# Three engines held to the order of the program in the main part of the second feed-forward layer

## The chip, the cores and the metric

One core of one Trainium2 chip runs the kernel. The metric is the device time of one execution in microseconds (us); several executions are timed, and one more is profiled. TensorE multiplies matrices, VectorE and ScalarE work on rows of 128 partitions, GpSimd helps a little at the start, and SyncE issues the DMA transfers. In the profile these are PE (with PEld, the load of weights), DVE, ACT, POOL and SP.

## What is computed

The input is a causal attention with exponential decay (2 batches, 8 heads, 768 positions, head dimension 64). Its output, as 1536 tokens of 512 features, goes through two feed-forward layers with 2048 hidden features each:

```
h = x @ w_in                       # layer 1
g = h * tanh(softplus(h))          # Mish
x = g @ w_out
h = x @ w2_in                      # layer 2
g = h * clip(h + 3, 0, 6) / 6      # hard swish
out = g @ w2_out
```

All is float32; the kernel splits each operand into a high and a low part and multiplies three times.

## The kernel before

**Layer 2** is what the change touches. It has three blocks of 512 tokens (in the order 2, 0, 1) and eight feature pieces `p` of 256 for each, so 24 steps `j` = 0 to 23. Both matrix products use a 2 x 2 block scheme with seven products in place of eight, which adds sums on VectorE. One step is the loop body over `j`, and it has four parts `f` = 0 to 3:

- `fill` (L687): the products of the first matrix for part `f`, into a PSUM bank: 6 matmuls of 256 columns for part 0 and 12 for each other part. I call them fill a, b, c and d. In steps 0 and 1 two banks take turns; from step 2 on all four fills use **one bank**, number 0.
- the copy out of that bank on ScalarE (L802), called copy a, b, c and d. The next fill can start only when the copy has read the bank.
- adds on VectorE with that copy (L805 in part 1, L809 and L812 in part 2, L814 in part 3).
- `second(j - 2)` (L701): products of the second matrix for the step two earlier, into other banks: 6 matmuls in part 0, 12 in each other part. In steps 0 and 1 the last matmuls of layer 1 (L327) stand here, and VectorE adds their results to `part` (L365).

Between these stand, for the features of step `j - 1`:

- `gate` (L711 on ScalarE, a relu into a buffer `x`; L712 on VectorE). It comes twice a step: for two of the four features at the end of a step (part 3), for the other two in part 0 of the next step.
- `feature_sums` (L721): four sums on VectorE, in part 0.
- `feature_parts`: two splits, each a high part on ScalarE (L88) and a low part on VectorE (L91), of 768 and of 1024 columns, in part 1. `second` reads them one step later.

**Tokens.** The sums over the tokens of the next block are a generator `token_sums` with seven splits (`put`: L88 on ScalarE, L91 on VectorE, 512 columns) and four differences (L383 on VectorE). The program takes one item of it in part 1 and one in part 3 of each step, from step 0 on for block 0 and from step 9 on for block 1.

**Closing.** With the last piece of a block, `close` (L737 on ScalarE, L740 and L745 on VectorE) scales and adds the seven accumulators and stores the result. That is in steps 9 and 17, and after step 23.

**What sets the order.** The tile framework orders each engine's instructions itself, by what it takes to be ready first, and an instruction can so be put ahead of one that the program has before it. An instruction that goes through `tc.keep_in_program_order` keeps its place in the program on its engine. Before the change only some instructions of the start do so. Each engine runs its queue in the order in which it was built.

Of the kernel before, what the change touches and what calls it, by code (L numbers as in the profile page):

```python
# [20 lines left out]
def decay_attention__mish_ffn__hswish_ffn_kernel(  # L21
# [14 lines left out]
    NPAIR = NF // 2  # L36

# [49 lines left out]
    def split_hi(hi, src):  # L87
        nc.scalar.activation(out=hi, in_=src, func=ACTF.Copy)  # L88

    def split_lo(lo, hi, src):  # L90
        nc.vector.tensor_tensor(out=lo, in0=src, in1=f32(hi), op=ALU.subtract)  # L91
# [43 lines left out]
    def decay_tables():  # L135
        small = tm1_p.tile([128, 344], F32, tag="th", name="small")
        tc.keep_in_program_order(nc.sync.dma_start(out=small[:, 0:140], in_=lam))
        load_raw(0, 0)
        load_raw(0, 1)
        load_raw(1, 0)  # L140
        load_w(*plan[0])
        load_raw(1, 1)
        unit, zero = small[:, 12:140], small[:, 144:272]
        nc.vector.memset(zero, 0.0)
# [12 lines left out]

    def scores(c, kind):
        qT, kT = qk(c)
        sc = [bank(kind, [128, 4, 128]) for h2 in range(2)]  # L160
        for p in range(4):
            for h2 in range(2):
                r = slice(h2 * 64, h2 * 64 + 64)
                nc.tensor.matmul(sc[h2][:, p, :], lhsT=kT[r, p, :], rhs=qT[r, p, :], start=True, stop=True)  # L164
        sc_t[c] = sc
# [7 lines left out]
    def weigh(c):  # L173
        qT, kT = qk(c)
        kn, vn = kv(c)
        sc = sc_t.pop(c)
        if c < 4:
            if carries(c):
                kk = kn.rearrange("j (p h d) -> j p h d", p=4, h=2)
                nc.gpsimd.tensor_tensor(out=kk, in0=kk, in1=reverse(), op=ALU.mult)  # L180
            if follows(c):
                nc.gpsimd.tensor_tensor(out=qT, in0=qT, in1=lampow, op=ALU.mult)
        else:
            lo = 0 if follows(c) else 1
            hi = 2 if carries(c) else 1
            qkn = raw_t[c][:, 512 + 512 * lo:512 + 512 * hi].rearrange("p (n i) -> p n i", i=512)
            nc.vector.tensor_tensor(out=qkn, in0=qkn, in1=table[:, lo:hi], op=ALU.mult)
        for h2 in range(2):
            nc.vector.tensor_tensor(out=amat[h2], in0=sc[h2], in1=mask[:, h2], op=ALU.mult)  # L189

    def attend(c, kind):
        qT, kT = qk(c)
        kn, vn = kv(c)
        uo = [bank(kind, [128, 2, 256]) for i in range(2)]
        u = uo[0][:, 1].rearrange("p (a d) -> p a d", a=4)
        o = [b[:, 0].rearrange("p (a i) -> p a i", a=2) for b in uo]
        half = [slice(0, 64), slice(64, 128)]
        if carries(c):
            for p in range(4):
                for h2 in range(2):  # L200
                    s = slice(p * 128 + h2 * 64, p * 128 + h2 * 64 + 64)
                    nc.tensor.matmul(u[half[h2], p], lhsT=kn[:, s], rhs=vn[:, s], start=True, stop=True)
        last = not follows(c)
        for h2 in range(2):
            for a in range(2):
                for e in range(2):
                    p = 2 * a + e
                    s = slice(p * 128 + h2 * 64, p * 128 + h2 * 64 + 64)
                    nc.tensor.matmul(  # L209
                        o[h2][half[e], a], lhsT=vn[:, s], rhs=amat[h2][:, p, :],  # L210
                        start=(a == 0), stop=(last and a == 1), skip_group_check=True,
                    )
        if follows(c):
            for a in range(2):
                for e in range(2):
                    for h2 in range(2):
                        p = 2 * a + e
                        nc.tensor.matmul(  # L218
                            o[h2][half[e], a], lhsT=state[c % 2][half[h2], p, :], rhs=qT[half[h2], p, :],
                            start=False, stop=(a == 1), skip_group_check=True,  # L220
                        )
        uo_t[c] = u, o
        del raw_t[c]

    def settle(c):
        u, o = uo_t.pop(c)
        off = (c % 4) * 128

        def tokens():
            for h2 in range(2):  # L230
                kt = slice(2 * h2, 2 * h2 + 2)
                hi = X[c // 4][:, 0, kt, off:off + 128]
                split_hi(hi, o[h2])
                split_lo(X[c // 4][:, 1, kt, off:off + 128], hi, o[h2])

        if c == 3:
            tokens()
        if carries(c):
            new = state[(c + 1) % 2]
            if follows(c):  # L240
                nc.vector.tensor_tensor(out=new, in0=faded, in1=u, op=ALU.add)
            else:
                nc.vector.tensor_copy(new, u)
            if carries(c + 1):
                nc.gpsimd.tensor_tensor(
                    out=faded, in0=new, in1=lampow[:, :, 127:128].to_broadcast([128, 4, 64]), op=ALU.mult
                )
        if c != 3:
            tokens()
# [31 lines left out]
    def to_single(st, dest=None):  # L281
# [7 lines left out]
        nc.vector.scalar_tensor_tensor(  # L289
            out=lo, in0=hi, scalar=-2 ** 31, in1=lo, op0=ALU.bitwise_and, op1=ALU.bitwise_or  # L290
        )
        nc.vector.scalar_tensor_tensor(  # L292
            out=hi if dest is None else dest.bitcast(I32), in0=hi, scalar=3, in1=lo,
            op0=ALU.logical_shift_left, op1=ALU.bitwise_or
        )
# [19 lines left out]
    def gemm1(k, t, h):  # L315
        order = [(kt, a, 0) for kt in range(4) for a in range(2)] + [(kt, 0, 1) for kt in range(4)]
        for kt, a, b in order:
            nc.tensor.matmul(  # L318
                h, lhsT=W[t][:, a, kt * 128:kt * 128 + 128], rhs=X[k][:, b, kt, :],
                start=(kt, a, b) == order[0], stop=(kt, a, b) == order[-1],  # L320
            )

    def gemm2(layer, t, g, y, first, last, es):
        for e in es:
            for i, (a, b) in enumerate(PASS):
                l, r = W[t][:, a, 512 + e * 128:640 + e * 128], g[:, b, :]
                nc.tensor.matmul(  # L327
                    y[e], lhsT=l, rhs=r, start=(first and i == 0), stop=(last and i == 2),
                )
# [13 lines left out]
    def act_first(n):  # L343
# [3 lines left out]
        nc.scalar.activation(out=x, in_=h, func=ACTF.Mish)  # L347
        nc.scalar.activation(out=g[:, 0], in_=h, func=ACTF.Mish)  # L348
# [9 lines left out]
    def evacuate(n, es):  # L358
        layer, k, t, first, last, end = seq[n]
        for e in es:  # L360
            y = y_t[e]
            if end == "keep":
                nc.scalar.activation(out=part[k][:, e, :], in_=y, func=ACTF.Copy)
            elif end == "add":
                nc.vector.tensor_tensor(out=part[k][:, e, :], in0=part[k][:, e, :], in1=y, op=ALU.add)  # L365
        if end == "split":
# [3 lines left out]
            nc.scalar.activation(out=tmp[:, 0], in_=y[:, 0:2, 256:512], func=ACTF.Copy)  # L370
# [3 lines left out]
    def token_sums(k, y, tmp=None):  # L374
# [7 lines left out]
        def sub(o, a, b):  # L382
            nc.vector.tensor_tensor(out=o, in0=a, in1=b, op=ALU.subtract)  # L383
# [121 lines left out]
    def assemble(u):  # L505
# [4 lines left out]
        for o, x, y, op in WSUMS[half]:  # L510
            nc.vector.tensor_tensor(out=B[:, o], in0=B[:, x], in1=B[:, y], op=op)
# [29 lines left out]
    for c in range(4):  # L541
# [12 lines left out]
        else:  # L554
            nc.gpsimd.tensor_copy(table[:, 1].rearrange("j (p h d) -> j p h d", p=4, h=2), reverse())
# [123 lines left out]
    def fill(j, ms, bank_):  # L679
        k, p = runs[j]  # L680
        slot = slot_at[j][p, 0]
        for i, m in enumerate(ms):
            wi, xi = FIRST[m]
            w, x = operand(slot, wi), XC[k][xi]
            for kt in range(2):
                for q, (a, b) in enumerate(PASS):
                    nc.tensor.matmul(  # L687
                        bank_[:, 256 * i:256 * i + 256], lhsT=w[:, a, kt * 128:kt * 128 + 128], rhs=x[:, b, kt],
                        start=(i == 0 and kt == 0 and q == 0), stop=(kt == 1 and q == 2), skip_group_check=True,
                    )  # L690

    def second(j, ms):
# [3 lines left out]
        for m in ms:  # L696
            gi, wi = SECOND[m]
            w, acc = operand(slot, wi), BANK[:, ACC[m]].rearrange("p (s n) -> p s n", s=2)
            for i in range(2):
                for q, (a, b) in enumerate(PASS):  # L700
                    nc.tensor.matmul(  # L701
                        acc[:, i], lhsT=GB[j % 2][:, gi, a, i * 128:i * 128 + 128], rhs=w[:, b],
                        start=(first and i == 0 and q == 0), stop=(last and q == 2), skip_group_check=True,
                    )
# [3 lines left out]
    def gate(j, lo, step):  # L708
        F = FH[j % 2][:, lo:lo + step + 1:step]
        x = tm2_p.tile([128, 2, 256], F32, tag="x", name="x")  # L710
        nc.scalar.activation(out=x, in_=F, func=ACTF.Relu, bias=3.0)  # L711
        nc.vector.scalar_tensor_tensor(out=F, in0=x, scalar=6.0, in1=F, op0=ALU.min, op1=ALU.mult)  # L712

    def feature_sums(j):
        F, S = FH[j % 2], FS[j % 2]
        A21, A11, A22, A12 = (F[:, i] for i in range(4))
        for o, a, b, op in (
# [3 lines left out]
            nc.vector.tensor_tensor(out=S[:, o], in0=a, in1=b, op=op)  # L721
# [14 lines left out]
    def scaled(o, m):  # L736
        nc.scalar.activation(out=o, in_=BANK[:, ACC[m]], func=ACTF.Copy, scale=SIXTH)  # L737

    def added(o, m, b):
        nc.vector.scalar_tensor_tensor(  # L740
            out=o, in0=BANK[:, ACC[m]], scalar=SIXTH, in1=b, op0=ALU.mult, op1=ALU.add
        )

    def plus(o, a, b):
        nc.vector.tensor_tensor(out=o, in0=a, in1=b, op=ALU.add)  # L745
# [40 lines left out]

    GAPS = ((1,), (4, 2), (6, 7), (5, 3))
    prepare = []
    for j in range(R):
# [7 lines left out]
        for f, (name, ms) in enumerate(FILLS):  # L797
# [4 lines left out]
            nc.scalar.activation(out=c, in_=bank_[:, 0:n], func=ACTF.Copy)  # L802
            c = c.rearrange("p (i n) -> p i n", n=256)
            if f == 1:
                nc.vector.tensor_tensor(  # L805
                    out=F[:, 2:4], in0=COPY["a"].unsqueeze(1).to_broadcast([128, 2, 256]), in1=c, op=ALU.add
                )
            elif f == 2:
                nc.vector.tensor_tensor(  # L809
                    out=F[:, 0:4:3], in0=F[:, 3:4].to_broadcast([128, 2, 256]), in1=c, op=ALU.add  # L810
                )
                nc.vector.tensor_tensor(out=F[:, 1], in0=F[:, 0], in1=c[:, 1], op=ALU.add)  # L812
            elif f == 3:
                nc.vector.tensor_tensor(out=F[:, 0:4:3], in0=F[:, 0:4:3], in1=c, op=ALU.add)  # L814
# [78 lines left out]
```

## Time and profile before

| | |
|---|---|
| three timed runs | 573.69, 572.15 and 571.12 us, median 572.15 us |
| the profiled execution | 571.27 us, of which the span of the trace is 569.5 us |
| mean granted TensorE clock | 0.999 |
| layer 2, step 0 starts | 311.72 us |
| PE busy, all instructions | 554.4 us, 97% of the span |
| DVE, ACT busy | 433.9 us (76%), 320.1 us (56%) |

The span runs from the first to the last instruction of the trace; the rest of the 571.27 us lies around it.

### The profile page before, as it was taken

Reading aid. Unit: us, or ns where it says so; the run is one execution under the profiler, and the core shown is the slowest. Engines: PE = TensorE matmul, PEld = TensorE weight load, DVE = VectorE, ACT = ScalarE, POOL = GpSimd, SP = SyncE. Lnnn points to the kernel's source line nnn. Section 1 sums busy time; section 2 is a strip of 40 time slices with the busy share of each in tenths; the row PEclk is TensorE's granted clock in tenths of the full one; section 3 lists DMA queues with packets and bytes.
Section 4 is the critical chain, followed back from the end, with each engine's and each line's share of the span. In section 5 each row is a group of like instructions: output and inputs, shape, how many; then the busy total and the mean of one; then the engine's idle time right before and its main releaser. Section 6 shows DMA issues by size and latency. Waiting matters only on the chain.

```text
span 569.5 us, 9630 instructions
## 1 busy us (share of the span) xinstructions
PE 554.4 (97%) x3886; PEld 492.0 (86%) x3886; DVE 433.9 (76%) x667; ACT 320.1 (56%) x476; POOL 16.7 (3%) x20
## 2 busy tenths in 40 slices
PE   7799999999999999999999999999999999999996
PEld 4677787778888888888888999999999999999995
DVE  6899953475637888798997696689887776987765
ACT  1578733346754676676765464465555555555451
POOL 3500100000000000000000000000000000000000
PEclk9999999999999999999999999999999999999999
DMA  8966612522355797869969999894498885699902
GB/s 307 401 220 246 245 66 75 185 75 94 134 181 210 291 386 263 346 234 399 389 277 393 402 360 378 325 351 168 164 364 322 314 330 174 219 346 347 381 34 74
DMA packets 25260, 149.06 MB, mean 262 GB/s; under 512 B 2304, under 2 KB 5504, under 8 KB 18304
## 3 DMA queue, kind: packets, MB, share of 16 engines
q1 hardware_dynamic: 25216, 148.45, 68.7%
q8 instruction: 30, 0.49, 0.3%
q14 instruction: 14, 0.11, 0.1%
HBM read 115.94 MB, written 32.51 MB: 261 GB/s over the span
## 4 chain that ended last, share of the span: by engine, by line
PE 85%; DVE 7%; ACT 3%; DMA 3%; issue 1%; SPq 0%; DVEq 0%; ACTq 0%
PE bank L318 22%; PE bank L327 21%; PE bank L687 20%; PE bank L701 18%; DMA st<-w 1%; DMA ring<-w 1%; PE bank L164 1%; PE bank L209 1%; PE bank L218 1%; DVE st L289 1%; DVE ring L292 1%; DVE amat L189 1%; ACT st L286 1%; DVE rest L740 1%; DVE X L91 1%
## 5 line engine op out<-in xcount | busy, mean ns | idle before, releaser
L327 PE MATMUL bank<-g,up 128*128 128x512 f32 x288 | 70.3, 389 | 0.0
L318 PE MATMUL bank<-X,up 128*128 128x512 f32 x288 | 69.2, 389 | 0.0
L347 ACT ACTIVATE x<-bank 128x512 f32<-128x512 f32 x48 | 28.6, 595 | 63.6 <-PE bank L318 63.5
L318 PEld LDWEIGHTS bank<-X,up 128*128 128x128 f32 x288 | 54.1, 188 | 11.2
L327 PEld LDWEIGHTS bank<-g,up 128*128 128x128 f32 x288 | 53.5, 188 | 10.6
L687 PE MATMUL bank<-X,up 128*128 128x256 f32 x384 | 55.5, 286 | 0.6 <-ACT work L802 0.5
L91 DVE TENSOR_TENSOR g<-x,g 128x512 fp32r<-128x512 f32 x48 | 32.9, 686 | 28.9 <-ACT g L348 28.7
L712 DVE SCALAR_TENSOR_TENSOR work<-x,work 128x512 f32<-128x512 f32 x48 | 33.1, 690 | 26.4 <-ACT x L711 26.3
L711 ACT ACTIVATE x<-work 128x512 f32<-128x512 f32 x48 | 30.3, 632 | 40.6 <-DVE work L812 24.6
L687 PEld LDWEIGHTS bank<-X,up 128*128 128x128 f32 x384 | 49.6, 191 | 1.5 <-ACT work L802 1.0
L802 ACT ACTIVATE two<-bank 128x512 f32<-128x512 f32 x48 | 28.6, 597 | 34.0 <-PE bank L687 34.0
L286 ACT ACTIVATE ring<-ring 128x512 f32<-128x512 f32 (+3 forms) x52 | 39.9, 818 | 13.5 <-DMA ring<-w 12.9
L318 PE MATMUL bank<-X,lowA 128*128 128x512 f32 x180 | 45.2, 397 | 0.0
L327 PE MATMUL bank<-g,lowA 128*128 128x512 f32 x180 | 43.2, 389 | 0.0
L701 PE MATMUL bank<-up,lowB 128*128 128x256 f32 x318 | 42.9, 283 | 0.0
L701 PEld LDWEIGHTS bank<-up,lowB 128*128 128x128 f32 x318 | 40.2, 192 | 0.0
L318 PEld LDWEIGHTS bank<-X,lowA 128*128 128x128 f32 x180 | 33.0, 188 | 8.2 <-issue 1.2
L687 PE MATMUL bank<-X,lowA 128*128 128x256 f32 x270 | 38.9, 285 | 1.2 <-ACT work L802 1.1
L327 PEld LDWEIGHTS bank<-g,lowA 128*128 128x128 f32 x180 | 33.8, 188 | 7.1
L802 ACT ACTIVATE work<-bank 128x256 f32<-128x256 f32 (+1 forms) x48 | 23.5, 490 | 27.7 <-PE bank L687 27.4
L701 PE MATMUL bank<-up,up 128*128 128x256 f32 x276 | 37.7, 283 | 0.0
L687 PEld LDWEIGHTS bank<-X,lowA 128*128 128x128 f32 x270 | 35.1, 191 | 2.1 <-ACT work L802 1.8
(103 smaller groups left out, 1018.7 us busy)
## 6 DMA issues: line engine op xcount, KB each, us to landing
up<-wc SPq DMA_DIRECT2D x19, 1792.0 KB, 10.1
wc<-lowA SPq DMA_DIRECT2D x16, 1792.0 KB, 8.9
lowA<-wc SPq DMA_DIRECT2D x13, 1792.0 KB, 8.4
raw<-att SPq DMA_DIRECT2D x24, 512.0 KB, 6.4
ring<-w SPq DMA_DIRECT2D x18, 512.0 KB, 5.1
ring<-w SPq DMA_DIRECT2D x8, 1024.0 KB, 5.7
spare<-w SPq DMA_DIRECT2D x8, 1024.0 KB, 6.3
lowB<-wc SPq DMA_DIRECT2D x6, 1280.0 KB, 5.8
```

The costliest lines, as they stand in the source:

```text
L91: nc.vector.tensor_tensor(out=lo, in0=src, in1=f32(hi), op=ALU.subtract)
L164: nc.tensor.matmul(sc[h2][:, p, :], lhsT=kT[r, p, :], rhs=qT[r, p, :], start=True, stop=True)
L189: nc.vector.tensor_tensor(out=amat[h2], in0=sc[h2], in1=mask[:, h2], op=ALU.mult)
L286: ins = nc.scalar.activation(out=o, in_=i, func=ACTF.Copy, scale=scale, bias=bias)
L318: nc.tensor.matmul(h, lhsT=W[t][:, a, kt * 128:kt * 128 + 128], rhs=X[k][:, b, kt, :], start=(kt, a, b) == order[0], stop=(kt, a, b) == or ...
L327: nc.tensor.matmul(y[e], lhsT=l, rhs=r, start=(first and i == 0), stop=(last and i == 2),)
L347: nc.scalar.activation(out=x, in_=h, func=ACTF.Mish)
L687: nc.tensor.matmul(bank_[:, 256 * i:256 * i + 256], lhsT=w[:, a, kt * 128:kt * 128 + 128], rhs=x[:, b, kt], start=(i == 0 and kt == 0 and ...
L701: nc.tensor.matmul(acc[:, i], lhsT=GB[j % 2][:, gi, a, i * 128:i * 128 + 128], rhs=w[:, b], start=(first and i == 0 and q == 0), stop=(las ...
L711: nc.scalar.activation(out=x, in_=F, func=ACTF.Relu, bias=3.0)
L712: nc.vector.scalar_tensor_tensor(out=F, in0=x, scalar=6.0, in1=F, op0=ALU.min, op1=ALU.mult)
L802: nc.scalar.activation(out=c, in_=bank_[:, 0:n], func=ACTF.Copy)
```

## The change

A set `held` of engine names is empty until just ahead of the loop over the 24 steps, and then gets three names. A helper `hold` sends an instruction through `tc.keep_in_program_order` where its engine is in the set. All the compute instructions of the kernel are wrapped in it; no instruction is added or taken away, and the order of the program in the text is the same. Seven lines are added ahead of the functions and one ahead of the loop, so line numbers of the changed kernel are 7 higher in `fill` and `second` (L694, L708) and 8 higher in the loop (L810 and on). The other wraps are like the two shown.

```
+    held = set()
+
+    def hold(engine, ins):
+        if engine in held:
+            tc.keep_in_program_order(ins)
+        return ins
+
...
-        nc.scalar.activation(out=hi, in_=src, func=ACTF.Copy)
+        hold("scalar", nc.scalar.activation(out=hi, in_=src, func=ACTF.Copy))
...
-            if dest is not None:
+            if dest is not None or "scalar" in held:
                 tc.keep_in_program_order(ins)
...
+    held.update(("tensor", "vector", "scalar"))
     GAPS = ((1,), (4, 2), (6, 7), (5, 3))
     prepare = []
     for j in range(R):
...
-            nc.scalar.activation(out=c, in_=bank_[:, 0:n], func=ACTF.Copy)
+            hold("scalar", nc.scalar.activation(out=c, in_=bank_[:, 0:n], func=ACTF.Copy))
```

The queues of SyncE and GpSimd are the same in both kernels. On TensorE two stretches differ: steps 4 and 5, and step 7. In step 4 before, fill a (6) and the first 3 matmuls of fill b stand ahead of the 6 matmuls of `second`:

```order
L687 MATMUL bank<-X_79,lowA 128x256 x9
L701 MATMUL bank<-lowA,lowB 128x256 x6
L687 MATMUL bank<-X_79,lowA 128x256 x3
L687 MATMUL bank<-lowA 128x256 x6
L701 MATMUL bank<-lowA,lowB 128x256 x12
```

In the changed kernel the same matmuls of step 4 stand so, `second` whole between fill a and fill b:

```order
L694 MATMUL bank<-X_79,lowA 128x256 x6
L708 MATMUL bank<-lowA,lowB 128x256 x6
L694 MATMUL bank<-X_79,lowA 128x256 x6
L694 MATMUL bank<-lowA 128x256 x6
L708 MATMUL bank<-lowA,lowB 128x256 x12
```

Three (step 5: eight, step 7: all twelve) matmuls of fill b moved behind `second`. On ScalarE the whole of layer 2 differs. Before, copies c and d of step 1 and copy a of step 2 (`work` 128x256) stand ahead of both relus (L711) of step 1's features:

```order
L802 ACTIVATE two<-bank 128x512 x2
L802 ACTIVATE work<-bank 128x256
L711 ACTIVATE x<-work 128x512 x2
L802 ACTIVATE work<-bank 128x512
L88 ACTIVATE up_1210<-work 128x3x256
```

In the changed kernel, at the same place, one relu (L718) and a split of a token item (`put`, L95 `X_77<-part`) stand ahead of copy a (L810 `work` 128x256):

```order
L810 ACTIVATE two<-bank 128x512 x2
L718 ACTIVATE x<-work 128x512
L95 ACTIVATE X_77<-part_768 128x512
L810 ACTIVATE work<-bank 128x256
L718 ACTIVATE x<-work 128x512
L810 ACTIVATE work<-bank 128x512
L95 ACTIVATE up_1210<-work 128x3x256
L95 ACTIVATE up_1210<-FS_2609 128x4x256
```

The token items moved here from layer 1, where before they had all been put, and copy a moved behind a relu. On VectorE, around the closing of the first block (`rest`, end of step 9 and start of step 10), the order before is:

```order
L809 TENSOR_TENSOR work<-work,two 128x2x256
L740 SCALAR_TENSOR_TENSOR rest<-bank,rest 128x512
L812 TENSOR_TENSOR work<-work,two 128x256
L740 SCALAR_TENSOR_TENSOR rest<-bank,rest 128x512
L745 TENSOR_TENSOR rest<-rest 128x512
L712 SCALAR_TENSOR_TENSOR work<-x,work 128x512
L745 TENSOR_TENSOR rest<-rest 128x512
L814 TENSOR_TENSOR work<-work,two 128x2x256
L740 SCALAR_TENSOR_TENSOR rest<-bank,rest 128x512 x3
L712 SCALAR_TENSOR_TENSOR work<-x,work 128x2x256
L805 TENSOR_TENSOR work<-work 128x512
L721 TENSOR_TENSOR FS_2609<-work 128x256 x2
```

In the changed kernel it is (L747 and L752 close, L719 gates, L390 is a token difference, L728 a feature sum):

```order
L817 TENSOR_TENSOR work<-work,two 128x2x256
L820 TENSOR_TENSOR work<-work,two 128x256
L747 SCALAR_TENSOR_TENSOR rest<-bank,rest 128x512 x2
L752 TENSOR_TENSOR rest<-rest 128x512 x2
L822 TENSOR_TENSOR work<-work,two 128x2x256
L747 SCALAR_TENSOR_TENSOR rest<-bank,rest 128x512 x3
L719 SCALAR_TENSOR_TENSOR work<-x,work 128x512
L390 TENSOR_TENSOR part_769<-part_769 128x2x256
L719 SCALAR_TENSOR_TENSOR work<-x,work 128x2x256
L728 TENSOR_TENSOR FS_2609<-work 128x256 x2
```

Both gates moved behind the whole closing, and a token difference came between them. On ScalarE of step 10, copy c before stands ahead of the 1024-column split; in the changed kernel it stands behind both splits, as in every step.

## Rows read from the trace of the kernel before

**Rows 1.** The page, part 1: busy us, share of the span, instructions.

```profile
PE 554.4 (97%) x3886; PEld 492.0 (86%) x3886; DVE 433.9 (76%) x667; ACT 320.1 (56%) x476; POOL 16.7 (3%) x20
```

**Rows 2.** Waits of TensorE's weight loads after 310 us: total, times, longest.

```profile
PEld bank L687 <- ACT work L802: 2.8, 5, 0.7
PEld bank L701 <- DVE up L91: 0.4, 1, 0.4
```

**Rows 3.** Timeline: start, duration, engine; a steady step, its copy a, the next.

```profile
441.74 0.88 PE L687 MATMUL bank<-X,up 128*128 128x256 f32 x6
442.46 0.88 PE L701 MATMUL bank<-lowB,up 128*128 128x256 f32 x6
442.72 0.39 ACT L802 ACTIVATE work<-bank 128x256 f32<-128x256 f32 x1 [0.17 <-PE bank L687]
451.90 0.88 PE L687 MATMUL bank<-X,up 128*128 128x256 f32 x6
```

**Rows 4.** Timeline: fill a of steps 4, 5, 8 and 10, fill b of 4.

```profile
347.47 0.88 PE L687 MATMUL bank<-X,lowA 128*128 128x256 f32 x6
348.88 0.62 PE L687 MATMUL bank<-X,lowA 128*128 128x256 f32 x3 [0.53 <-ACT work L802]
358.33 0.88 PE L687 MATMUL bank<-X,up 128*128 128x256 f32 x6
...
390.20 0.94 PE L687 MATMUL bank<-X,lowA 128*128 128x256 f32 x6
...
411.35 0.88 PE L687 MATMUL bank<-X,lowB 128*128 128x256 f32 x6
```

**Rows 5.** Timeline of the tail: the last wait of TensorE.

```profile
559.69 4.33 PE L701 MATMUL bank<-lowA,up 128*128 128x256 f32 x34 [0.17 <-DVE up L91]
```

**Rows 6.** Timeline of steps 0 to 2: fills, VectorE, ScalarE.

```profile
318.10 0.88 PE L687 MATMUL bank<-X,lowA 128*128 128x256 f32 x6
...
323.76 0.88 PE L687 MATMUL bank<-X,lowA 128*128 128x256 f32 x6
324.05 0.42 DVE L721 TENSOR_TENSOR FS<-work,FS 128x256 f32<-128x256 f32 x1
...
324.39 0.68 DVE L805 TENSOR_TENSOR work<-work 128x512 f32<-128x512 f32 x1
...
324.51 1.06 ACT L88 ACTIVATE lowB<-FS 128x1024 fp32r<-128x1024 f32 x1 [0.73 <-DVE FS L721]
...
325.47 0.58 ACT L802 ACTIVATE two<-bank 128x512 f32<-128x512 f32 x1
...
327.30 0.87 PE L687 MATMUL bank<-X,up 128*128 128x256 f32 x6
```

**Rows 7.** Busy us (x instructions) of each engine, clock, DMA share, 321 to 337.

```profile
321.00:337.00 16.00, 16.00 (x127) 15.61 (x126) 15.67 (x28) 9.87 (x15) 0.00 (x0) 1.00 0.99 417
```

**Rows 8.** Groups by line, shapes apart: busy us, mean ns, idle before.

```profile
L712 DVE SCALAR_TENSOR_TENSOR work<-x,work 128x512 f32<-128x512 f32 x48 | 33.1, 690 | 26.4 <-ACT x L711 26.3
L711 ACT ACTIVATE x<-work 128x512 f32<-128x512 f32 x48 | 30.3, 632 | 40.6 <-DVE work L812 24.6 <-DVE work L814 15.6
L802 ACT ACTIVATE two<-bank 128x512 f32<-128x512 f32 x48 | 28.6, 597 | 34.0 <-PE bank L687 34.0
L721 DVE TENSOR_TENSOR FS<-work 128x256 f32<-128x256 f32 x48 | 18.2, 421 | 0.7
L805 DVE TENSOR_TENSOR work<-work 128x512 f32<-128x512 f32 x24 | 16.6, 690 | 6.2 <-ACT work L802 6.2
L91 DVE TENSOR_TENSOR up<-FS,up 128x1024 fp32r<-128x1024 f32 x12 | 14.7, 1225 | 4.2 <-ACT up L88 4.2
L91 DVE TENSOR_TENSOR up<-work,up 128x768 fp32r<-128x768 f32 x12 | 11.4, 951 | 0.0
L740 DVE SCALAR_TENSOR_TENSOR rest<-bank,rest 128x512 f32<-128x512 f32 x16 | 10.3, 683 | 1.7 <-PE bank L701 1.6
L383 DVE TENSOR_TENSOR part<-part 128x512 f32<-128x512 f32 x8 | 5.5, 684 | 0.0
```

More of the change, by code (lines that the diff above doesn't have):

```diff
@@ L105, in warm_up @@
         for _ in range(count):
-            nc.tensor.matmul(wp, lhsT=wz[:, 0:128], rhs=wz, start=True, stop=True)
+            hold("tensor", nc.tensor.matmul(wp, lhsT=wz[:, 0:128], rhs=wz, start=True, stop=True))
     pinned = [True]
@@ L143, in decay_tables @@
         unit, zero = small[:, 12:140], small[:, 144:272]
[L144 removed]
+        hold("vector", nc.vector.memset(zero, 0.0))
         def powers(o, i, first, drive):
@@ L163, in scores @@
                 r = slice(h2 * 64, h2 * 64 + 64)
-                nc.tensor.matmul(sc[h2][:, p, :], lhsT=kT[r, p, :], rhs=qT[r, p, :], start=True, stop=True)
+                hold("tensor", nc.tensor.matmul(sc[h2][:, p, :], lhsT=kT[r, p, :], rhs=qT[r, p, :], start=True, stop=True))
         sc_t[c] = sc
@@ L201, in attend @@
                     s = slice(p * 128 + h2 * 64, p * 128 + h2 * 64 + 64)
-                    nc.tensor.matmul(u[half[h2], p], lhsT=kn[:, s], rhs=vn[:, s], start=True, stop=True)
+                    hold("tensor", nc.tensor.matmul(u[half[h2], p], lhsT=kn[:, s], rhs=vn[:, s], start=True, stop=True))
         last = not follows(c)
@@ L217, in attend @@
                         p = 2 * a + e
-                        nc.tensor.matmul(
+                        hold("tensor", nc.tensor.matmul(
                             o[h2][half[e], a], lhsT=state[c % 2][half[h2], p, :], rhs=qT[half[h2], p, :],
                             start=False, stop=(a == 1), skip_group_check=True,
-                        )
+                        ))
         uo_t[c] = u, o
@@ L240, in settle @@
             if follows(c):
-                nc.vector.tensor_tensor(out=new, in0=faded, in1=u, op=ALU.add)
+                hold("vector", nc.vector.tensor_tensor(out=new, in0=faded, in1=u, op=ALU.add))
             else:
-                nc.vector.tensor_copy(new, u)
+                hold("vector", nc.vector.tensor_copy(new, u))
             if carries(c + 1):
-                nc.gpsimd.tensor_tensor(
+                hold("gpsimd", nc.gpsimd.tensor_tensor(
                     out=faded, in0=new, in1=lampow[:, :, 127:128].to_broadcast([128, 4, 64]), op=ALU.mult
-                )
+                ))
         if c != 3:
@@ L317, in gemm1 @@
         for kt, a, b in order:
-            nc.tensor.matmul(
+            hold("tensor", nc.tensor.matmul(
                 h, lhsT=W[t][:, a, kt * 128:kt * 128 + 128], rhs=X[k][:, b, kt, :],
                 start=(kt, a, b) == order[0], stop=(kt, a, b) == order[-1],
-            )
+            ))
     def gemm2(layer, t, g, y, first, last, es):
@@ L326, in gemm2 @@
                 l, r = W[t][:, a, 512 + e * 128:640 + e * 128], g[:, b, :]
-                nc.tensor.matmul(
+                hold("tensor", nc.tensor.matmul(
                     y[e], lhsT=l, rhs=r, start=(first and i == 0), stop=(last and i == 2),
-                )
+                ))
     lower, upper = range(0, HALF), range(HALF, NF)
@@ L346, in act_first @@
         x = tm2_p.tile([128, 512], F32, tag="x", name="x")
-        nc.scalar.activation(out=x, in_=h, func=ACTF.Mish)
-        nc.scalar.activation(out=g[:, 0], in_=h, func=ACTF.Mish)
+        hold("scalar", nc.scalar.activation(out=x, in_=h, func=ACTF.Mish))
+        hold("scalar", nc.scalar.activation(out=g[:, 0], in_=h, func=ACTF.Mish))
         f_t[n] = x
@@ L362, in evacuate @@
             if end == "keep":
-                nc.scalar.activation(out=part[k][:, e, :], in_=y, func=ACTF.Copy)
+                hold("scalar", nc.scalar.activation(out=part[k][:, e, :], in_=y, func=ACTF.Copy))
             elif end == "add":
-                nc.vector.tensor_tensor(out=part[k][:, e, :], in0=part[k][:, e, :], in1=y, op=ALU.add)
+                hold("vector", nc.vector.tensor_tensor(out=part[k][:, e, :], in0=part[k][:, e, :], in1=y, op=ALU.add))
         if end == "split":
@@ L369, in evacuate @@
             tmp = ring[:, 2].bitcast(F32).rearrange("p (i e n) -> p i e n", i=2, e=2)
-            nc.scalar.activation(out=tmp[:, 0], in_=y[:, 0:2, 256:512], func=ACTF.Copy)
+            hold("scalar", nc.scalar.activation(out=tmp[:, 0], in_=y[:, 0:2, 256:512], func=ACTF.Copy))
             for _ in token_sums(k, y, tmp):
@@ L382, in sub @@
         def sub(o, a, b):
-            nc.vector.tensor_tensor(out=o, in0=a, in1=b, op=ALU.subtract)
+            hold("vector", nc.vector.tensor_tensor(out=o, in0=a, in1=b, op=ALU.subtract))
         def put(i, src):
@@ L510, in assemble @@
         for o, x, y, op in WSUMS[half]:
-            nc.vector.tensor_tensor(out=B[:, o], in0=B[:, x], in1=B[:, y], op=op)
+            hold("vector", nc.vector.tensor_tensor(out=B[:, o], in0=B[:, x], in1=B[:, y], op=op))
         ready[u] = B[:, 1:8]
@@ L720, in feature_sums @@
         ):
-            nc.vector.tensor_tensor(out=S[:, o], in0=a, in1=b, op=op)
+            hold("vector", nc.vector.tensor_tensor(out=S[:, o], in0=a, in1=b, op=op))
     def feature_parts(j):
```

58 lines of the change are left out of this document (29 added, 29 removed).

## Prediction

> **What bounds the kernel now.** I read the page first: TensorE (PE) is busy for 97% of the span, VectorE for 76%, ScalarE for 56% [rows 1]. So TensorE's own time is the floor, and only its waits can be won or lost. The view of waits names those in layer 2: 2.8 us of weight loads wait for ScalarE's copy out of the fill bank (L802), 0.4 us for VectorE [rows 2]. The timeline shows where. In a steady step fill a begins at 441.74 and the next step's at 451.90: 10.16 us for 84 matmuls [rows 3]. Six matmuls take 0.72 us (441.74 to 442.46), 0.12 each, so 84 take 10.08; 0.08 is lost behind copy a, which starts 0.98 after fill a does, that is 0.26 after its last matmul was due to end its turn, and takes 0.39. That small loss comes from TensorE's own pace and stays.
>
> Three steps are longer. Step 4 takes 358.33 − 347.47 = 10.86 us, and steps 5 and 7, which the change shows with the same order, take as long; in step 4 the matmuls of fill b wait for copy a until 348.88, with `second` queued behind them [rows 4]. Steps 8 and 9 take 411.35 − 390.20 = 21.15 together, 0.83 more than two steady ones [rows 4].
>
> How the side engines work I take from steps 0 to 2. An independent VectorE instruction starts 0.08 before its forerunner's recorded end (324.05 + 0.42 against 324.39), a dependent one 0.04 after the end (ScalarE's split at 324.51 after 324.47). ScalarE's next independent one starts 0.10 early (325.47 against 324.51 + 1.06) [rows 6]. The same rows show what a fixed order costs: copy c of step 1 had its matmuls at 323.76 + 0.88 = 324.64, but began at 325.47, because the split ahead of it in ScalarE's queue had itself waited 0.73 us for VectorE [rows 6]. There it cost nothing, since two banks take turns in steps 0 and 1. From step 2 on one bank serves, and each such delay past the matmuls of `second` stops TensorE.
>
> **What the change removes.** Nothing is added; every duration stays. With `second` back between fill a and fill b, steps 4, 5 and 7 fall to 10.16: 3 x 0.70 = 2.1 us. In steps 8 and 9, before, token items and relus stand close ahead of copies; I take the whole 0.83 as won, and count what the new order costs there below. In the tail, TensorE continues at 559.69 after 0.17 of wait on the low part of the last split, some 0.3 with the weight load of [rows 2, 5]; VectorE now ends all four sums before the 768-column part, so the 1024-column part comes 0.8 earlier (one 0.95 less overlap) and the 0.3 goes. Together 3.2 us.
>
> **What it adds: three blocks.** Durations are those of [rows 8]; L809, L814, L365 and the token's L91 are taken as the 0.69 and 0.68 of the rows of their size, L812 as the sum of 256 columns, 0.42, a `put` on ScalarE as a relu, 0.63, L737 as copy c, 0.60.
>
> Block one, start of step 2. The token items now lie in steps 0 to 5 and the four adds of layer 1 in steps 1 and 2, just where VectorE is full already: 15.67 of 16 us busy [rows 7]. In the new order VectorE runs L814, L712, L383, L365, L712, four L721, L805, L365, two L91, L383, L809, L812: 16 instructions, 5 x 0.69 + 4 x 0.68 + 4 x 0.42 + 0.95 + 1.22 + 0.42 = 10.44, less 12 overlaps of 0.08, plus 3 gaps of 0.04: 9.60 us. Fill d of step 0 ends at 318.98 [rows 6]; copy d starts 0.10 later, as copy a does [rows 3], takes 0.60, so the chain runs from 319.72 to 329.32. ScalarE's relu of part 3 needs L812: 329.36 to 329.99; the `put` behind it ends at 330.52, and copy a of step 2, queued behind both, at 330.81. Fill b, due at 327.30 + 1.44 = 328.74, starts at 330.85: 2.1 us. Before, copy a stood ahead of the relu.
>
> Block two, step 10. In step 9 the closing puts L737 ahead of the relu. From that step's fill a: copy a 0.98 to 1.37, L737 at 1.44 + 0.26 = 1.70 to 2.30, relu to 2.83, gate to 3.56, four sums to 5.16, L805 from 5.08. From there VectorE runs 21 instructions to the last sum of step 10 (L805, two L91, a token's L91, L809, L812, two L740, two L745, L814, three L740, L712, L383, L712, four L721): 5 x 0.69 + 9 x 0.68 + 0.95 + 1.22 + 0.42 + 1.68 = 13.84, less 15 overlaps, plus 5 gaps: 12.84, so to 17.92. The 1024-column split (1.06) follows to 19.02, copy c behind it to 19.52. Fill d of step 10 is due at 10.16 + 0.1 (copy c of step 9, behind a `put`, comes that late) + 0.08 + 7.20 = 17.54. It starts at 19.56: 2.0 us, and the 0.1.
>
> Block three, step 18: the same without the token's two instructions, 1.20 earlier: 18.36 against 17.44, 0.9 us.
>
> In the other steps the new order fits: without L737 the relu follows copy a at 1.27 and the sums end at 4.2; copy b (3.14 to 3.74) and the two splits (0.85 and 1.06) free ScalarE by 5.5, and copy c can't start before 0.08 + 5.76 + 0.26 = 6.1. Sum of the blocks 5.1, net 5.1 − 3.2 = **+1.9 us**. On the profiled execution's own 571.27 that gives 573.2; on the median of the timed runs, 572.15, which lies 0.9 higher, 574.0. I forecast **573.6 us**, +1.9 being 0.3%, which is under the 0.5% (2.9 us) that a measurement of this kernel can tell from no change.
>
> Unknown costs have bounds. A block can cost nothing, if VectorE comes in time, or the chain without any overlap: 12, 15 and 13 overlaps of 0.08 are 1.0, 1.2 and 1.0 more. I take the overlaps as they stand, since [rows 6] shows them in a full stretch. What token items free in layer 1 I count as nothing: TensorE's idle time of the whole span, 15 us [rows 1], is work that VectorE's late part of layer 1 doesn't hold; at most it is some tenths. DMA issues keep their order; each waits for a slot's last matmul, so it moves with TensorE, and the DMA share of 0.99 in 321 to 337 [rows 7] left TensorE no wait for a transfer [rows 2].
>
> **Rivals.** (1) *The order on the side engines costs nothing*: only the 3.2 us are seen, 571.27 − 3.2 = 568.1. For it: VectorE's 76% and ScalarE's 56%. The Trainium skill (Perfetto Trace Analysis, section Identifying the Most-Contended Engine) says that for these engines occupancy is a fair measure of how close they are to their limit; by that alone, VectorE has a quarter to spare and this rival would be the forecast. Against it: the share is a mean over stages, and the stage that counts is full [rows 7]; the trace so does not bear the rule out for a single stretch. Chance 0.08.
>
> (2) *The blocks are longer*, and the kernel measurably slower: with no overlap on VectorE +3.2, so 571.27 + 1.9 + 3.2 = 576.4. It decides from 1.0 us more over the 56 chained instructions, 0.02 each. For it: waits on two semaphores now stand in one queue, and one late link moves all behind it. Against it: pace and gaps of [rows 6]. Chance 0.27.
>
> (3) *The order of TensorE gives nothing back*: if `second` in steps 4, 5 and 7 itself had to wait for weights, the 2.1 would stay lost, 573.2 + 2.1 = 575.3. Against it: in step 4 before, it ran right after 348.88 with no wait of its own [rows 2, 4]. Its chance of 0.05 is within the 0.27.
>
> **How the numbers follow.** Forecast 0.65, rival 1 0.08, rival 2 with 3 0.27. The likeliest case alone spans 571.9 to 575.0. The range of 571.0 to 576.4 leaves out rival 1's full gain and little above. Faster by over 0.5%: 0.08; within: 0.65; slower: 0.27.
>
> **What would show it.** In the profile after: steps 4, 5 and 7 at 10.2 us; step 2 near 12.2 with copy a behind a relu that waited for L820; step 10 near 12.1 and step 18 near 11.1 with copy c behind the split L95 that waited for L728; TensorE's waits for L810 near 5 us plus 0.08 a step. I am wrong if these three steps are near 10.2, or if further steps, 3 or 11 above all, carry the lateness on.

## The result, and the profile after

| | before | after |
|---|---|---|
| median of the timed runs | 572.47 us (5 runs, 571.12 to 573.69) | 575.78 us (5 runs, 574.20 to 576.41) |
| the profiled execution, its span | 571.27, 569.5 us | 576.41, 574.6 us |
| its mean granted clock | 0.999 | 0.995 |

The ratio of the times is 1.0062, with a 95% interval of 1.0042 to 1.0082: the changed kernel is slower, by 3.3 us between the medians. (The ratio is the recorded one and not the quotient of the two medians, 1.0058; that holds for the ratios of the experiments too.) The range held the time. The likeliest case, a difference that can't be told from none, did not come; the case given 0.27 did.

First the page, then the waits of TensorE's weight loads after 300 us, for the kernel after:

```profile
PE 556.2 (97%) x3886; PEld 493.8 (86%) x3886; DVE 432.1 (75%) x667; ACT 311.6 (54%) x476; POOL 16.6 (3%) x20
```

```profile
PEld bank L694 <- ACT two L810: 2.8, 2, 2.0
PEld bank L694 <- ACT work L810: 2.1, 1, 2.1
```

The page says nothing of the change beside [rows 1]: no share moved by more than two points. PE's busy time even grew by 1.8 us with the same 3886 matmuls, and that will matter below. The waits say more. In [rows 2] stand five for the copies, of at most 0.7 us, and one of 0.4 for VectorE; the same view has one more of 0.2, for a copy into `two`, which makes 3.4 us. In the kernel after they are three, of up to 2.1, 4.9 us together, and none is for VectorE.

**Where the 5.1 us of the two profiled executions lie.** Not all are the change's. Step 0 starts at 311.72 before and at 313.45 after, 1.73 later. These two windows, first of the kernel before, then of the one after, show how early that arose (columns as in [rows 7]):

```profile
0.00:60.00 60.00, 53.22 (x520) 39.57 (x520) 52.07 (x85) 35.86 (x58) 13.61 (x17) 1.00 0.81 299
60.00:300.00 240.00, 239.08 (x1276) 195.35 (x1276) 176.53 (x247) 143.26 (x203) 3.10 (x4) 1.00 0.60 225
```

```profile
0.00:60.00 60.00, 52.32 (x513) 38.40 (x514) 50.11 (x83) 34.63 (x56) 12.88 (x16) 1.00 0.80 285
60.00:300.00 240.00, 239.07 (x1276) 195.20 (x1275) 173.45 (x241) 140.14 (x199) 3.71 (x4) 1.00 0.61 227
```

By 60 us the kernel after had run 7 matmuls less; from there to 300 both ran 1276. In the first 60 us the two kernels have the same instructions in the same order, and in the profiles of this study step 0 starts anywhere from 311.7 to 314.9; three experiments whose layer 1 is that of the kernel after start it at 311.79 to 312.21. So the 1.73 is put down to the execution, and layer 2 is compared from step 0 to the end of the span: 574.6 − 313.45 = 261.15 us against 569.5 − 311.72 = 257.78. The difference, **+3.37 us**, is that of the medians (3.3).

**Layer 2 step by step.** The timeline of after: TensorE in steps 2 to 5 and 10, with the instructions of ScalarE and VectorE that the prediction named, and the tail:

```profile
329.03 0.87 PE L694 MATMUL bank<-X,up 128*128 128x256 f32 x6
330.50 0.42 DVE L820 TENSOR_TENSOR work<-work,two 128x256 f32<-128x256 f32 x1
331.02 0.63 ACT L718 ACTIVATE x<-work 128x512 f32<-128x512 f32 x1 [1.82 <-DVE work L820]
331.56 0.61 ACT L95 ACTIVATE X<-part 128x512 fp32r<-128x512 f32 x1
332.08 0.36 ACT L810 ACTIVATE work<-bank 128x256 f32<-128x256 f32 x1
332.49 1.06 PE L694 MATMUL bank<-X,up 128*128 128x256 f32 x6 [1.87 <-ACT work L810]
333.35 1.49 PE L694 MATMUL bank<-lowA,up 128*128 128x256 f32 x6
334.64 2.49 PE L708 MATMUL bank<-up,lowB 128*128 128x256 f32 x12
336.96 0.88 PE L694 MATMUL bank<-lowA,up 128*128 128x256 f32 x6
342.71 0.88 PE L694 MATMUL bank<-X,lowB 128*128 128x256 f32 x6
352.87 0.88 PE L694 MATMUL bank<-X,lowA 128*128 128x256 f32 x6
363.02 0.88 PE L694 MATMUL bank<-X,up 128*128 128x256 f32 x6
...
413.82 0.88 PE L694 MATMUL bank<-X,lowB 128*128 128x256 f32 x6
420.98 0.42 DVE L728 TENSOR_TENSOR FS<-work,FS 128x256 f32<-128x256 f32 x1
421.44 1.06 ACT L95 ACTIVATE up<-FS 128x1024 fp32r<-128x1024 f32 x1 [0.74 <-DVE FS L728]
422.40 0.58 ACT L810 ACTIVATE two<-bank 128x512 f32<-128x512 f32 x1
423.03 0.98 PE L694 MATMUL bank<-X,lowB 128*128 128x256 f32 x6 [1.78 <-ACT two L810]
426.01 0.88 PE L694 MATMUL bank<-X,lowA 128*128 128x256 f32 x6
...
563.91 5.20 PE L708 MATMUL bank<-lowA,up 128*128 128x256 f32 x42
```

The chains are there as they were forecast. In step 2 the relu (L718) waits for L820, the `put` of a token item (L95 `X<-part`) follows, then copy a, and fill b starts 332.49 − (329.03 + 1.44) = 2.02 after it was due. In step 10 the 1024-column split waits for the last sum (L728), copy c waits behind it, and TensorE stands idle for 1.78 ahead of fill d. Step 4 takes 363.02 − 352.87 = 10.15, and the tail shows no wait where [rows 5] had one.

But step 2 lasts 342.71 − 329.03 = 13.68 us, not 12.2. The row at 334.64 shows why: 12 matmuls take 336.96 − 334.64 = 2.32 us, 0.19 each in place of 0.12, and nothing is waited for. The windows of after around both waits (the number ahead of the last two is the granted clock):

```profile
329.00:333.00 4.00, 2.13 (x17) 1.89 (x16) 3.97 (x8) 2.13 (x5) 0.00 (x0) 1.00 1.04 440
333.00:337.00 4.00, 4.00 (x23) 4.00 (x23) 3.93 (x9) 2.07 (x3) 0.00 (x0) 0.57 1.00 423
421.00:425.00 4.00, 2.22 (x19) 2.02 (x18) 4.00 (x6) 1.71 (x3) 0.00 (x0) 1.00 0.48 175
```

Behind the wait of step 2, TensorE's granted clock is 0.57 as a mean over 4 us; within them it stood at 0.50, the lower of its two levels (1.2 of 2.4 GHz). That takes 4 x (1 − 0.57) = 1.7 us, near the 13.68 − 10.08 − 2.02 = 1.58 by which the step is longer than its 84 matmuls of 0.12 and its wait. It counts as busy time, hence the 1.8 us more of PE on the page. Behind the wait of step 10, nearly as long, the clock stayed at 1.00.

| layer 2 | forecast, us | measured, us |
|---|---|---|
| step 2: fill b waits for copy a | +2.1 | +2.02 |
| step 2: half clock behind it | not seen | +1.58 |
| step 10: fill d waits for copy c | +2.0 | +2.04 (12.19 − 10.15) |
| step 18: the same | +0.9 | +0.87 (11.02 − 10.15) |
| steps 4, 5 and 7 | −2.1 | −2.12 (to 10.15 each) |
| steps 8 and 9 | −0.83 + 0.1 | −0.81 (10.15 and 10.19) |
| steps 3, 11 and 19 | 0 | +0.19 (10.09 to 10.15 each) |
| from fill a of step 23 to the end | −0.3 | −0.41 |
| sum | +1.9 | +3.37 (of the unrounded rows) |

### The profile page after: what moved, and what is told of

It reads as the page before. It is cut to its first block, busy times and chain, and to the rows that moved or that the text cites. A ratio compares the mean times of both kernels' runs of the same rounds, so it can differ in the third digit from the quotient of the medians.

```text
span 574.6 us, 9660 instructions
## 1 busy us (share of the span) xinstructions
PE 556.2 (97%) x3886; PEld 493.8 (86%) x3886; DVE 432.1 (75%) x667; ACT 311.6 (54%) x476; POOL 16.6 (3%) x20
## 4 chain that ended last, share of the span: by engine, by line
PE 80%; DVE 8%; DMA 6%; ACT 3%; issue 2%; SPq 1%; DVEq 0%; ACTq 0%
PE bank L334 21%; PE bank L325 20%; PE bank L708 18%; PE bank L694 18%; DMA st<-w 5%; DMA raw<-att 2%; DVE rest L747 2%; ACT st L293 1%; DVE FS L728 1%; PE bank L171 1%; PE bank L216 1%; DVE work L719 1%; DVE lowB L98 1%; PE bank L225 1%; DVE rest L752 1%
## 5 line engine op out<-in xcount | busy, mean ns | idle before, releaser
L334 PEld LDWEIGHTS bank<-g,up 128*128 128x128 f32 x288 | 53.5, 188 | 10.6
L810 ACT ACTIVATE two<-bank 128x512 f32<-128x512 f32 x48 | 28.6, 596 | 58.6 <-PE bank L694 58.2
L694 PE MATMUL bank<-X,up 128*128 128x256 f32 x384 | 55.6, 286 | 1.9 <-ACT work L810 1.9
L694 PEld LDWEIGHTS bank<-X,up 128*128 128x128 f32 x384 | 49.6, 191 | 2.4 <-ACT work L810 2.1
L810 ACT ACTIVATE work<-bank 128x256 f32<-128x256 f32 (+1 forms) x48 | 23.5, 491 | 50.8 <-PE bank L694 50.6
L719 DVE SCALAR_TENSOR_TENSOR work<-x,work 128x512 f32<-128x512 f32 x48 | 32.9, 688 | 19.6 <-ACT x L718 19.5
L708 PE MATMUL bank<-up,lowB 128*128 128x256 f32 x318 | 43.7, 287 | 0.0
L708 PEld LDWEIGHTS bank<-up,lowB 128*128 128x128 f32 x318 | 41.2, 197 | 0.0
L325 PEld LDWEIGHTS bank<-X,lowA 128*128 128x128 f32 x180 | 33.0, 188 | 9.5 <-issue 1.2
L694 PE MATMUL bank<-X,lowA 128*128 128x256 f32 x270 | 38.8, 285 | 0.0
L822 DVE TENSOR_TENSOR work<-work,two 128x512 f32<-128x512 f32 x24 | 16.6, 691 | 28.3 <-ACT two L810 28.2
L708 PE MATMUL bank<-up,up 128*128 128x256 f32 x276 | 37.7, 283 | 0.0
L98 DVE TENSOR_TENSOR lowA<-spare,lowA 128x1792 fp32r<-128x1792 f32 x16 | 32.3, 2018 | 5.5 <-ACT lowA L95 5.5
```

The costliest lines, as they stand in the source:

```text
L98: hold("vector", nc.vector.tensor_tensor(out=lo, in0=src, in1=f32(hi), op=ALU.subtract))
L325: hold("tensor", nc.tensor.matmul(h, lhsT=W[t][:, a, kt * 128:kt * 128 + 128], rhs=X[k][:, b, kt, :], start=(kt, a, b) == order[0], stop=( ...
L334: hold("tensor", nc.tensor.matmul(y[e], lhsT=l, rhs=r, start=(first and i == 0), stop=(last and i == 2),))
L694: hold("tensor", nc.tensor.matmul(bank_[:, 256 * i:256 * i + 256], lhsT=w[:, a, kt * 128:kt * 128 + 128], rhs=x[:, b, kt], start=(i == 0 a ...
L708: hold("tensor", nc.tensor.matmul(acc[:, i], lhsT=GB[j % 2][:, gi, a, i * 128:i * 128 + 128], rhs=w[:, b], start=(first and i == 0 and q = ...
L719: hold("vector", nc.vector.scalar_tensor_tensor(out=F, in0=x, scalar=6.0, in1=F, op0=ALU.min, op1=ALU.mult))
```

## The experiments

The experiments stand beside runs of the kernel before on the same chip: its median is 571.49 us (34 runs) for the first four and 572.72 us (20 runs) for the others. Length of steps is from fill a to the next fill a in the profiled execution.

### TensorE alone in program order

```
-    held.update(("tensor", "vector", "scalar"))
+    held.update(("tensor",))
```

> Only TensorE is held to the order of the program; VectorE and ScalarE are ordered freely, as before. If the gain of the change is TensorE's own order, as the prediction has it, steps 4, 5 and 7 fall from 10.86 to about 10.2 us and no block appears in steps 2, 10 and 18: 2.1 us less than before, ratio 0.996. Rival: the free order of ScalarE was laid out for a TensorE that lets its second product wait in these steps, and puts copy b or c behind a split there; then steps 4, 5 and 7 stay at 10.9 or get longer, and the ratio is 1.000 to 1.003.

Measured: 574.75 us, ratio 1.0041 (1.0022 to 1.0061), against 0.996 expected. Holding TensorE alone gives nothing back; it costs, as the rival had it, and more than the rival's 1.003. Steps 4, 5 and 7 took 11.35, 11.34 and 11.66 us, longer than before (10.86 in step 4, [rows 4]), and no other step gained. Step 4 in the timeline, ScalarE and TensorE:

```profile
352.40 1.06 ACT L95 ACTIVATE up<-FS 128x1024 fp32r<-128x1024 f32 x1 [1.49 <-DVE FS L728]
353.36 0.58 ACT L810 ACTIVATE work<-bank 128x512 f32<-128x512 f32 x1
354.00 0.98 PE L694 MATMUL bank<-lowA 128*128 128x256 f32 x6 [0.94 <-ACT work L810]
```

ScalarE's free order has the 1024-column split ahead of copy b, and the split waits for VectorE's last sum. Before, part of fill b ran ahead of `second`, and no wait for copy b stood in these steps, only the 0.53 for copy a [rows 4]. So the 2.1 us that these steps win in the changed kernel need ScalarE's order as much as TensorE's.

### VectorE and ScalarE in program order, TensorE free

```
-    held.update(("tensor", "vector", "scalar"))
+    held.update(("vector", "scalar"))
```

> VectorE and ScalarE are held, TensorE is ordered freely. If the loss lies in the order of the side engines: step 2 at 13.7 us with the clock at half rate behind its wait, step 10 at about 12, step 18 at about 11, and steps 4, 5 and 7 still at 10.9 or more, so 4 to 6 us over before, ratio 1.007 to 1.010, the slowest of the three. Rival (the loss comes with TensorE's new order): ratio 1.000 or below.

Measured: 575.15 us, ratio 1.0058 (1.0041 to 1.0076): slower than before, but under the 1.007 expected, and no slower than the change. The waits of weight loads:

```profile
PEld bank L694 <- ACT work L810: 4.1, 8, 0.9
PEld bank L694 <- ACT two L810: 0.9, 4, 0.2
```

The one long wait and the half clock that were expected in step 2 did not come. The waits are cut up: twelve, none over 0.9. TensorE's queue, ordered by the framework, has `second` ahead of the late fills (21 matmuls between fill a and fill b in step 2), so TensorE works while ScalarE is late, and the clock stays at 1.00 through layer 2 up to its last matmul. The waits in steps 4, 5 and 7 stay, 0.53 and more. Layer 2 is 2.6 us longer in this profile (575.3 − 314.88 against 257.78). The weight loads wait 5.0 us against 3.4 before, which accounts for 1.6 of it; the cause of the rest is not shown. By steps, 2 and 3 together are 1.4 us longer than before, step 7 is 1.0, 10 and 11 together are 1.0, and 18 and 19 together 0.5; 0.8 is won in steps 8 and 9 and 0.4 behind the start of step 23. So the side engines' order has a price of its own, with TensorE's order or without.

### The 1024-column split behind copy c

```
-    def feature_parts(j):
+    def feature_parts(j, which=(0, 1)):
         F, S, G = FH[j % 2], FS[j % 2], GB[j % 2]
-        split(G[:, 0:3, 0], G[:, 0:3, 1], F[:, 1:4])
-        split(G[:, 3:7, 0], G[:, 3:7, 1], S)
+        if 0 in which:
+            split(G[:, 0:3, 0], G[:, 0:3, 1], F[:, 1:4])
+        if 1 in which:
+            split(G[:, 3:7, 0], G[:, 3:7, 1], S)
...
-                feature_parts(j - 1)
+                feature_parts(j - 1, (0,))
+            elif f == 2 and j > 0:
+                feature_parts(j - 1, (1,))
```

> The change, but the program itself takes the 1024-column split in part 2, behind copy c, in place of part 1. If copy c waits because it stands behind that split in ScalarE's queue, the blocks of steps 10 and 18 shrink from 2.0 and 0.9 us to under 0.5 each, and block one shrinks too, for 1.2 us of VectorE work leave its chain: its wait is about 1 us and the clock stays at full rate. Some 4.5 us less than the change, 571.3 us, ratio to before 0.998. Rival (VectorE has too much work in these steps, whatever the order): steps 10 and 18 stay at 12.2 and 11.0, ratio 1.004 or more.

Measured: 571.9 us, ratio 0.9992 (0.9973 to 1.0011): the loss is gone. Step 18 fell from 11.02 to 10.15, step 10 from 12.19 to 10.43, with 0.49 of it coming back in step 11 (10.64). In step 10 copy c now goes ahead of the split, and fill d follows it:

```profile
416.33 0.58 ACT L812 ACTIVATE two<-bank 128x512 f32<-128x512 f32 x1
416.96 0.98 PE L694 MATMUL bank<-X,lowB 128*128 128x256 f32 x6
417.17 1.06 ACT L95 ACTIVATE up<-FS 128x1024 fp32r<-128x1024 f32 x1 [0.26 <-DVE FS L728]
```

So it was the split that held copy c back. The 0.76 that is left in steps 10 and 11 has other reasons: in step 10 the 768-column split still stands ahead of copy c, and in step 11 fill b waits 0.31 for copy a, which stands behind a relu and a `put`. Step 2 fell too, to 11.07, with TensorE waiting 0.74 for copy a in place of 1.87. That is one VectorE instruction less in its chain: the split's low part (1.22) now comes behind L820. The clock was 1.00 up to the last matmul of this execution.

### The same, and the token items two steps and one step later

```
         if j == 0:
             g_lo(STEPS - 1)
+        if j == 2:
             prepare.append(token_sums(0, part[0]))
-        if j == NPAIR + 1:
+        if j == NPAIR + 2:
             prepare.append(token_sums(1, part[1]))
```

> As the one before, and the token items begin two steps later (step 2 in place of 0, step 10 in place of 9), behind the full stretches; the same work in all. If the blocks are late links in a fixed order and nothing else, no step waits longer than the 0.08 us: the gain of 3.2 us alone remains, about 569.2 us, ratio 0.9945, below both kernels. Rival (token work that now lies in layer 2 costs time as such, 11 items of about 1.3 us on two engines): no lower than the run before it.

Measured: 570.43 us, ratio 0.9963 (0.9945 to 0.9982): faster than the kernel before, and so than the changed one. TensorE waits for nothing in layer 2, and steps 2 to 22 all take 10.14 to 10.16. The start of step 2 in the timeline:

```profile
326.88 0.42 DVE L823 TENSOR_TENSOR work<-work,two 128x256 f32<-128x256 f32 x1
327.48 0.87 PE L694 MATMUL bank<-X,up 128*128 128x256 f32 x6
327.54 0.62 ACT L718 ACTIVATE x<-work 128x512 f32<-128x512 f32 x1
328.45 0.38 ACT L813 ACTIVATE work<-bank 128x256 f32<-128x256 f32 x1 [0.29 <-PE bank L694]
328.91 0.96 PE L694 MATMUL bank<-X,up 128*128 128x256 f32 x6
```

L823 is the sum that was L820 in the changed kernel. It ends before fill a begins, the relu after it is over at 328.16, and copy a waits only for its matmuls. Layer 2 takes 566.6 − 311.9 = 254.7 us, 3.1 less than before: the prediction's 3.2 of gains, with none of the blocks. That is one profile each; the ratio is a gain of 2.1 us, and the medians lie 1.1 apart, so how much of the 3.1 a mean execution keeps is less sure than that there is a gain.

### The token items later, the split where it was

```
         if j == 0:
             g_lo(STEPS - 1)
+        if j == 2:
             prepare.append(token_sums(0, part[0]))
```

> The change, but the token items of block 0 begin in step 2 in place of step 0; all else as in the change. Two differences of 0.68 us on VectorE and a put of 0.63 on ScalarE leave the chain of block one. If the chain is what holds copy a, the wait in step 2 falls from 2.0 to about 0.7 us and the clock stays at full rate: step 2 at 10.8 in place of 13.7, 2.9 us less than the change, 572.9 us, ratio to before 1.001; steps 10 and 18 as in the change. Rival (the clock falls for another reason than the wait): step 2 still near 12.3.

Measured: 573.84 us, ratio 1.0018 (1.0002 to 1.0035). The median is 0.9 above the 572.9 expected. Step 2 took 10.74, with a wait of 0.43 (1.87 in the changed kernel); so the token items made most of block one. Step 18 was 11.03, as in the changed kernel. Step 10, which the edit doesn't touch, took 13.38, and the windows around its wait show the same thing as step 2 of the changed kernel did:

```profile
416.00:420.00 4.00, 2.21 (x18) 2.01 (x18) 3.97 (x8) 2.07 (x3) 0.00 (x0) 1.00 0.73 263
420.00:424.00 4.00, 4.00 (x23) 4.00 (x22) 3.41 (x6) 1.75 (x3) 0.00 (x0) 0.57 0.81 264
```

Fill d waited 1.79, 0.01 more than in the changed kernel, and here the clock was 0.57 behind it, where there it stayed at 1.00. The step is 13.38 − 12.19 = 1.19 longer, and step 11, whose fill a still runs at half clock (1.03 us in place of 0.72), 10.46 − 10.15 = 0.31: 1.50 together.

### Eight more matmuls in the wait of step 2

```
                 second(j - LAG, GAPS[f])
+                if j == 2 and f == 0:
+                    for _ in range(8):
+                        hold("tensor", nc.tensor.matmul(
+                            BANK[:, ACC[2]][:, 0:256], lhsT=GB[0][:, 0, 0, 0:128], rhs=GB[0][:, 0, 0],
+                            start=True, stop=True, skip_group_check=True,
+                        ))
```

The eight write a bank that a later matmul starts anew, so they add work and nothing else.

> The change, with 8 matmuls of 256 columns more in step 2 between second and fill b, whose result is overwritten; they run while TensorE waits for copy a, so they add work where there is none. If the half clock behind that wait comes from the idle time, the clock stays at 1.00 and step 2 takes about 12.2 in place of 13.7 us: 1.5 us less than the change, ratio to before 1.0035. Rival (the clock falls in any case, or the extra matmuls delay fill b): 1.006 to 1.008.

Measured: 575.13 us, ratio 1.0040 (1.0022 to 1.0058). The wait of step 2 and what is behind it, in windows:

```profile
331.00:333.00 2.00, 1.07 (x9) 0.87 (x8) 2.00 (x4) 1.81 (x4) 0.00 (x0) 1.00 1.02 437
333.00:337.00 4.00, 4.00 (x35) 4.00 (x35) 3.93 (x9) 2.33 (x4) 0.00 (x0) 1.00 1.01 427
```

Fill b starts as late as in the changed kernel (332.35 − 328.87 = 3.48 after fill a; 3.46 there), but TensorE idles 0.93 in place of 1.87. Behind that the clock stays at 1.00, and 35 matmuls touch the 4 us where 23 did. Step 2 takes 12.22: with more work in it, it is 1.46 us shorter. Steps 10 and 18 (12.20 and 11.03) are those of the changed kernel. That is what was expected if the half clock comes from the idle time, but it is one execution, and three waits of 1.7 to 1.8 us in these profiles (step 10 of this very run among them) had no half clock behind them either. So the link is likely and not shown; and the two ratios, 1.0040 and 1.0062, have intervals that overlap.

### TensorE with one of the side engines

```
+    held.update(("tensor", "scalar"))      # one kernel
+    held.update(("tensor", "vector"))      # the other
```

> TensorE and ScalarE are held, VectorE is free. If ScalarE's fixed order carries the loss by itself, the blocks of steps 2, 10 and 18 stay, and their size moves with what VectorE puts first: ratio 1.004 to 1.012. Rival (VectorE's fixed order carries it): no blocks, steps 4, 5 and 7 at 10.2, ratio 0.995.

> TensorE and VectorE are held, ScalarE is free. If ScalarE's fixed order carries the loss, the blocks are gone and the gain of steps 4, 5 and 7 stands: ratio 0.995. Rival: VectorE in a fixed order behind a ScalarE that is ordered by another plan makes new small waits, in steps 4 to 7 as in the run with TensorE alone and in steady steps: ratio 1.003 to 1.010.

Measured, without VectorE: 576.7 us, ratio 1.0065 (1.0042 to 1.0089). The three blocks stand: step 2 took 11.62, step 10 14.27 (a wait of 2.37, and the clock 0.50 to 0.54 in 422 to 425), step 18 12.09. The queues of TensorE and ScalarE are those of the changed kernel, and steps 4, 5 and 7 took 10.15. Copies behind a waiting relu or split are ScalarE's queue alone; VectorE's order sets only how late they come, and in steps 10 and 18 the free one was later, in step 2 it was earlier (1.29 of idle time in place of 1.87).

Measured, without ScalarE: 577.06 us, ratio 1.0080 (1.0058 to 1.0102), the slowest by its median. The blocks are gone (steps 2, 10 and 18: 10.23, 10.15, 10.15), but the split ahead of copy b costs again:

```profile
PE bank L694 <- ACT work L810: 4.1, 11, 0.9
```

Steps 4, 5 and 7 took 11.40, 11.30 and 11.13, with waits of 0.72 to 0.93. In eight further steps (8, 9, 15 to 17 and 21 to 23; the first seven take 10.6 us each) fill c waits 0.20 for copy b: I take it that ScalarE's free order, still the framework's, does not fit the times at which the held VectorE delivers the sums; that was not tried.

## Why the prediction was right, and where it was not

**What bounds the kernel** was read rightly: the change in layer 2 is made up of TensorE's waits, and of its clock, and VectorE's share, 75% after 76, told nothing of it.

**The gains** came as forecast, 3.3 of 3.2 us. The reason for the largest was incomplete: "With `second` back between fill a and fill b, steps 4, 5 and 7 fall to 10.16" holds only while ScalarE has copy b ahead of the split. TensorE's order alone made these steps 11.35 to 11.66; TensorE's and ScalarE's together gave the 10.15, with VectorE free.

**The three blocks** came at their places and in their size: 2.02, 2.04 and 0.87 us for 2.1, 2.1 (with the 0.1 in step 9) and 0.9. The chains can be checked link by link. From step 9's fill a at 403.63, the last sum ends at 421.40 (forecast 17.92 later, 421.55) and copy c at 422.98 (423.15). Moving the split away from copy c took block three whole, and block two but for 0.76 in steps 10 and 11; starting the token items later took 1.44 us of block one's wait of 1.87; both together left no wait.

**The step that failed** is the short sentence "Nothing is added; every duration stays." It was taken from a profile in which TensorE never stopped for more than 0.7 us in layer 2. The matmuls' 0.12 us is a duration at full clock, and behind the wait of step 2 the granted clock was 0.57 for 4 us: +1.58, about the whole distance from +1.9 to the measured +3.4. The term for it in the sum was nothing. In the run with eight added matmuls, which halved the idle time and left the lateness, there was none of it. So the kernel came out measurably slower, as rival 2 had it, by a mechanism that none of the rivals named: rival 2 wanted longer chains, and they were not longer. That 575.78 lies within the range is luck in that part: the room above 573.6 was there for longer chains. The 0.5% that a measurement was said to need was also too much: the interval of the ratio is 0.2% to either side, so that even the +1.9 us (0.33%) would have stood clear of it. Rival 1 is refuted, since the side engines' order alone costs 1.0058, and rival 3 too, since steps 4, 5 and 7 took 10.15.

**What stays open** is when the clock falls. Two waits of almost the same length (1.87 and 1.78) in one execution had it fall behind the first and not behind the second, and in the kernel with later token items it fell behind the second (1.79). Nor is it a cost of every execution to the same amount: the timed runs of the changed kernel have mean clocks of 0.991 to 0.998. Such losses are not the change's alone. A mean clock of 0.996 or less stands in 17 of the 30 executions of the four kernels that have a wait of 1.78 us or more, in 12 of the 51 of the other five experiments, and in 8 of the 54 of the kernel before beside the experiments. The first 60 us, the same instructions in the same order in all ten profiles, show it too: the clock fell there in two of them. The Trainium skill (TensorE: Matmul & The Clock Gate, What's actually happening) says that one kernel, run again, has a different number of matmuls at the low clock at its start. That the clock fell there in two profiles and not in eight agrees with it in kind; nothing here tried what decides it.

## What to carry to other kernels

A fixed order is as good as the program that is written down: before it is imposed, look in each queue for an instruction that frees a bank and stands behind one that waits for another engine, above all in stretches where that engine is full (15.67 of 16 us here), since the mean share won't show it. An order for some engines and not for the others was no halfway house, 1.0041 to 1.0080 in the four mixtures; moving the two late producers in the program gave 0.9963. When a new wait of TensorE of about 2 us enters a sum, price it twice: once as idle time, and once, as a possible extra, at half clock behind it (1.5 to 1.6 us here).

## What the runs showed of the hardware that was not expected

Six times in layer 2 TensorE stood idle for 1.68 to 2.37 us in these profiles. Three times the granted clock then fell to 0.50 once it worked again: step 2 of the changed kernel (1.87 us of idle time), step 10 with later token items (1.79) and step 10 without VectorE (2.37). In the first that took 1.58 us, in the second 1.50. Three times the clock stayed at 1.00: step 10 of the changed kernel and of the one with eight more matmuls (1.78 each) and step 18 without VectorE (1.68). Behind shorter idle times, up to 1.29, it did not fall in layer 2. That is no safe bound, though: at the start of the kernel, where the same instructions run in the same order, the clock fell at 24.45 us in the profile with TensorE free, behind idle times of 1.13 and 0.47, and stayed at 1.00 behind the same two (1.13 and 0.47; 1.12 and 0.47) in the kernels before and after.
